# Moving two splits behind an exponential, spreading a check of words, and putting one small product ahead of an output block, in a fused recurrence and feed-forward kernel

## The chip, the cores and the metric

The kernel runs on one core of a Trainium2 chip. The metric is the device time of one execution in microseconds (us). Before the change it takes 355.14 us (median of three runs, 355.14 to 355.28). All comparisons below are between runs that count as fast; a run of a program on one core counts as slow when it is over 1.5% above the fastest of its kernel.

Engines: TensorE (PE, its weight loads PEld), VectorE (DVE), ScalarE (ACT), GpSimd (POOL), SyncE (SP, which here issues nearly all DMAs). The granted clock is the share of TensorE's full clock that the profile records as granted.

## The reference, cut to what matters

```python
for t in range(S):                      # B,H,S,D = 4,8,768,48
    cur = einsum('bhd,bhe->bhde', u[None] * kt, vt)
    y[:, :, t] = einsum('bhd,bhde->bhe', rt, state + cur)
    state = w[None, :, :, None] * state + einsum('bhd,bhe->bhde', kt, vt)
x = y.transpose(0, 2, 1, 3).reshape(B * S, H * D)          # 3072 x 384
h = x @ w_in                                               # 384 -> 1024
e = exp(h - max(h)); sm = e / (sum(e) + 1e-9); solu = h * sm
ln = (solu - mean(solu)) / sqrt(var(solu) + 1e-6) * g_ln
out = ln @ w_out                                           # 1024 -> 384
```

The 3072 rows are cut into N = 24 chunks of 128. The weights come as 64-bit words. The kernel converts them on the chip in a short way that is right only for words of ordinary size, so it reads all words a second time, checks them, and at the end goes a slower general way if the verdict is bad.

Of the kernel before, what the change touches and what calls it, by code (L numbers as in the profile page):

```python
# [399 lines left out]
def direct_path(  # L400
# [64 lines left out]
    def load(i, which="krv"):  # L465
        b, c = units[i]
        for t, src, n in ((kpads, k, "k"), (rpads, r, "r"), (vts, v, "v")):
            if n in which:
                nc.sync.dma_start(out=t[i % len(t)][:, :, 0:D],
                                  in_=src[b, :, ts(c, T), :].rearrange("h s d -> s h d"))  # L470
# [133 lines left out]
    for j in range(8):  # L604
# [5 lines left out]
        else:  # L610
            n = 1 << (j - 1)
# [21 lines left out]
    N = len(units)  # L633
# [3 lines left out]
    def check_sums():  # L637


        L = len(pieces)  # L640
        good = small.tile([128, 2, N + L + HP], F32, name="good", bufs=1)
        low = small.tile([128, 1], F32, name="low", bufs=1)
        nc.vector.tensor_single_scalar(out=good[:, 0, :N], in_=sums, scalar=1.0 / MOST,
                                       op=ALU.is_ge)
        nc.vector.tensor_single_scalar(out=good[:, 1, :N], in_=sums, scalar=MOST, op=ALU.is_le)
        nc.vector.tensor_single_scalar(out=good[:, 0, N : N + L], in_=least, scalar=FLOOR, op=ALU.is_ge)
        nc.vector.tensor_single_scalar(out=good[:, 1, N : N + L], in_=total, scalar=CEIL, op=ALU.is_le)
        nc.vector.tensor_single_scalar(out=good[:, 0, N + L :], in_=decays, scalar=LOW,
                                       op=ALU.is_ge)
        nc.vector.tensor_single_scalar(out=good[:, 1, N + L :], in_=decays, scalar=HIGH,  # L650
                                       op=ALU.is_le)
        nc.vector.tensor_reduce(out=low, in_=good, axis=AX.XY, op=ALU.min)
        n_ps = psH.tile([128, dff], F32, tag="h", name="n_ps")[0:1, 0:1]
        nc.tensor.matmul(n_ps, low, ones, start=True, stop=True)
        nc.vector.tensor_single_scalar(out=bad, in_=n_ps, scalar=127.5, op=ALU.is_lt)
# [10 lines left out]
    def decay_k(i):  # L666
        X = live.setdefault(i, {})
        X["kp"] = apool.tile([128, H, P], F32, name="kp", bufs=5)
        nc.gpsimd.tensor_mul(X["kp"].rearrange("p h d -> p (h d)"),  # L669
                             kpads[i % NLD].rearrange("p h d -> p (h d)"),  # L670
                             kdec.rearrange("p a d -> p (a d)"))
# [78 lines left out]
    def heads(i):  # L750
        b, c = units[i]
        X = live[i]
        vt, AT, St = vts[i % NV], X["AT"], states[b]
        vf = vt.rearrange("p h d -> p (h d)")
        y_ps = psM.tile([128, KD, 128], F32, tag="m", name="y_ps")
        last = {m: n for n, (m, h, at) in enumerate(inner)}
        opened = set()

        def into(m, lhsT, rhs, stop):
            j, g = divmod(m, 4)  # L760
            nc.tensor.matmul(y_ps[32 * g : 32 * g + 32, j, :], lhsT, rhs, start=(g not in opened),  # L761
                             stop=stop, skip_group_check=True)
            opened.add(g)

        if c > 0:
            for m in range(12):
                a, n = divmod(m, 3)
                into(m, St[:, a].rearrange("p q d -> p (q d)")[:, ts(n, 32)], X["rT"][:, a, :],
                     False)
        for n, (m, h, at) in enumerate(inner):  # L770
            into(m, vf[:, at : at + 32], AT[:, h, :], last[m] == n)
        X["y"] = y_ps

    def take_y(i):
        X = live[i]
        X["xT"] = fpool.tile([128, KD, 128], F32, name="xT", bufs=LA + 1)
        nc.scalar.copy(out=X["xT"], in_=X["y"])  # L777

    def outer(chunks):

        chunks = [i for i in chunks if i < N and units[i][1] < C - 1]
        if not chunks:
            return
        kv_ps = psM.tile([128, 2, HP, D], F32, tag="m", name="kv_ps")
        for n, i in enumerate(chunks):
            X, vt = live[i], vts[i % NV]
            X["kv"] = kv_ps[:, n]
            for a in range(HP):
                for g in range(4):
                    h = 2 * a + g // 2  # L790
                    nc.tensor.matmul(X["kv"][ts(g, 32), a], X["kp"][:, h, ts(g % 2, 32)],  # L791
                                     vt[:, h, 0:D], start=True, stop=True)
# [39 lines left out]
    def deviation(i):  # L832
        ss, var, rstd = live[i]["st"]
        live[i]["rstd"] = rstd
        nc.gpsimd.tensor_scalar(out=var, in0=ss, scalar1=1.0 / dff, scalar2=1e-6 * dff ** 2,  # L835
                                op0=ALU.mult, op1=ALU.add)
        nc.gpsimd.tensor_tensor(out=rstd, in0=var, in1=neg_half, op=ALU.pow)
# [4 lines left out]
    def halves():  # L842

        return wpool.tile([128, 2 * 8 * 64, 1], U32, tag="raw", name="halves",
                          bufs=6).bitcast(U16).rearrange("p n o -> p (n o)")

    def split(words):
        return words.bitcast(U16).rearrange("p (n o) -> p o n", o=2)

    def turn(both):  # L850

        turned = halves()
        nc.sync.dma_start(out=turned.rearrange("p (n t) -> p n t", t=128), in_=both,
                          transpose=True)
        return turned.rearrange("p (o n t) -> p o n t", o=2, t=128)
# [5 lines left out]
    def halve_ln(i):  # L861
        X = live[i]
        both = halves()
        nc.scalar.copy(out=both.rearrange("p (o n) -> p o n", o=2), in_=split(X["solu"]))  # L864
        X["turned"] = turn(both)
# [6 lines left out]
    def halve_rk(i):  # L872
        if i < FIRST:
            return
        X = live[i]
        both = halves()
        parts = both.rearrange("p (o e n) -> p o e n", o=2, e=2)
        nc.scalar.copy(out=parts[:, :, 1], in_=split(X["kp"].rearrange("p h d -> p (h d)")))
        nc.vector.tensor_copy(out=parts[:, :, 0], in_=split(X["rp"].rearrange("p h d -> p (h d)")))
        X["turned"] = turn(both)  # L880

    def join_rk(i):
        X = factors(i)
        join(X["rk"].rearrange("p e a t -> p (e a) t"), X["turned"])
# [20 lines left out]
    now = []  # L905
    for i in range(-2, LA + LO):
# [8 lines left out]
        before, now = now, [todo.pop(0) for _ in range(conversions.get(i, 0))]  # L915
# [82 lines left out]
    for i in range(LA + LO, N + LA + LO, 2):  # L998
        j, l = i - LA, i - LA - LO
        for n in (i, i + 1):  # L1000
            if n + 5 < N:
                load(n + 5, "kr")
            if n + 3 < N:
                load(n + 3, "v")
        new = [n for n in (i + 1, i + 2) if FIRST <= n < N]
        late = i == LA + LO
        if late:
            ffn_in(j)
            unit(j)
        for n in (i + 3, i + 4):  # L1010
            if n < N:
                decay_k(n)
                decay_r(n)
                weigh(n, nc.gpsimd)
        for n in (j - 2, j - 1):
            if LO - 1 <= n < N:
                deviation(n)
        if l + 2 < N:
            halve_ln(l + 2)
        for n in new[:1]:  # L1020
            diagonal(n)
        join_ln(l + 1)
        for n in new[:1]:
            join_rk(n)
        if j < N and not late:
            ffn_in(j)
            unit(j)
        if i + 3 < N:
            halve_rk(i + 3)
        for n in new[1:]:  # L1030
            join_rk(n)
        check_next()
        ffn_out(l)
        if l + 3 < N:
            halve_ln(l + 3)
        if j + 1 < N:
            ffn_in(j + 1)
        for n in new[1:]:
            diagonal(n)
        if j + 1 < N:  # L1040
            unit(j + 1)
        if l + 1 == N - 1:
            check_sums()
        ffn_out(l + 1)
        if i + 4 < N:
            halve_rk(i + 4)
        for n in (i + 3, i + 4):
            if n < N:
                sum_own(n)
        now = [n for n in (i + 1, i + 2) if n < N]  # L1050
        for n in now:
            scores(n)
        for n in now:
            take_scores(n)
        now = [n for n in (i, i + 1) if n < N]
        for n in now:
            heads(n)
            take_y(n)
        outer(now)
        for n in now:  # L1060
            update(n)
        if l + 2 < N:
            join_ln(l + 2)
        if i >= N - 1:
            check_next()
    return bad

# [41 lines left out]
```

## The kernel before: the parts that the change touches

From chunk 7 on the chunks go in pairs: twelve iterations with i = 7, 9, ..., 29. In one iteration, rows (scores, y) are at chunks i and i+1, the first product h and its exponential at j = i - 2, and the second product o at l = i - 7. In the traces each engine's work stands in the order in which this loop writes it; in the changed kernel, a split for which ACT waited 3.08 us held up the exponential behind it. A split cuts the 32-bit values of a tile into 16-bit halves, a DMA transposes the halves into a second buffer ("turned"), and a join puts them together again. All these buffers come from one rotation of six.

```python
LA, LO, FIRST = 2, 5, 9
psH = tile_pool(name="psH", bufs=1, space=PSUM)   # h
psM = tile_pool(name="psM", bufs=2, space=PSUM)   # y, kv and o share two buffers

def ffn_in(i):                       # PE: 12 matmuls of 512 columns (h_ps); ACT: exponential
def unit(i):                         # DVE: reciprocal, h*e (solu); ACT: centre, square
def halves():                        # buffers for split words and for turned ones
    return wpool.tile(..., tag="raw", name="halves", bufs=6)
def halve_ln(i):                     # ACT: split rows of solu into 16-bit halves
    both = halves()
    nc.scalar.copy(out=both, in_=split(X["solu"]))
    X["turned"] = turn(both)         # SP: DMA transpose into another buffer
def join_ln(i):                      # DVE: joins the turned halves (lnT)
def halve_rk(i):                     # the same for k (ACT) and r (DVE)
def heads(i): ...                    # PE: y_ps of chunk i from scores and state
def take_y(i):                       # ACT: xT <- y_ps
def ffn_out(i):                      # PE: 16 matmuls (o_ps); ACT: o <- o_ps; SP: store
def check_next():                    # check the piece loaded last, load the next; 14 pieces
    for p in checked: check_words(p) # ACT: abs and its sum; DVE: least of it
    ...
def check_sums(): ...                # DVE: seven small operations; PE: n_ps; DVE: bad

for i in range(LA + LO, N + LA + LO, 2):
    j, l = i - LA, i - LA - LO
    late = i == LA + LO              # the first pair: ffn_in(j), unit(j) come first
    ...                              # cut: loads, decays on POOL, deviation
    if l + 2 < N: halve_ln(l + 2)
    ...                              # cut: diagonal, join_ln(l + 1), join_rk, ffn_in(j), unit(j)
    if i + 3 < N: halve_rk(i + 3)
    ...
    check_next()
    ffn_out(l)
    if l + 3 < N: halve_ln(l + 3)
    if j + 1 < N: ffn_in(j + 1)
    ...                              # cut: diagonal
    if j + 1 < N: unit(j + 1)
    if l + 1 == N - 1: check_sums()
    ffn_out(l + 1)
    if i + 4 < N: halve_rk(i + 4)
    ...                              # cut: scores, take_scores of i + 1, i + 2
    for n in (i, i + 1): heads(n); take_y(n)
    outer(now); update(n)            # kv_ps and the state
    if l + 2 < N: join_ln(l + 2)
    if i >= N - 1: check_next()
```

## Time and profile before

| | before |
|---|---|
| time | 355.14 us |
| TensorE busy | 335.1 us of 354.3 (95%) |
| ACT busy | 241.0 us (68%) |
| one pair in the middle | 26.60 us, TensorE busy for all of it |
| TensorE's waits after the start-up | 1.5 us (n_ps, the verdict), 0.8 us (y_ps), 0.6 us (h_ps), and 0.3 us (kv_ps) for nothing that the profile shows |

The table is read from the bottom up: an engine that is busy for the whole of a pair sets the time there, and the only time that an order of instructions can win is what this engine waits. The prediction shows the lines.

### The profile page before, as it was taken

What the parts mean: (1) busy time and instruction counts of PE and PEld (TensorE: products, weight loads), DVE (VectorE), ACT (ScalarE), POOL (GpSimd) and SP (SyncE); (2) the same over time, 40 slices, a digit from 0 to 9 for tenths busy, and PEclk for the clock granted to TensorE, in tenths of its full rate; (3) what the DMA queues carried; (4) which work ended last, traced back from release to release, by engine and by line L of the source; (5) the groups of instructions that cost most, each with busy time, mean ns of one, the idle gap of its engine ahead of it and who ended that gap; (6) DMA issues with size and microseconds to landing.
All of it is one profiled execution on the core that took longest, in us unless ns stands there. A gap on an engine that the chain in (4) does not pass through costs nothing.

```text
span 354.3 us, 8478 instructions
## 1 busy us (share of the span) xinstructions
PE 335.1 (95%) x3427; PEld 205.5 (58%) x3427; DVE 210.4 (59%) x347; ACT 241.0 (68%) x457; POOL 178.7 (50%) x196
## 2 busy tenths in 40 slices
PE   2699999999999999999999999999999999999983
PEld 2485566655655665575575575575565565555552
DVE  7795888887487468378378378378373252332330
ACT  3765988988878857867867866866867636547520
POOL 3879667789249449449449449449442000000000
PEclk9999999999999999999999999999999999999998
DMA  8999996259999798887999788772973422346941
GB/s 168 264 227 214 245 209 107 51 105 193 199 220 177 177 171 120 185 154 138 187 148 146 185 152 140 186 147 56 174 111 64 97 68 81 85 104 141 213 116 32
DMA packets 164877, 52.76 MB, mean 149 GB/s; under 512 B 157916, under 2 KB 161244, under 8 KB 164828
## 3 DMA queue, kind: packets, MB, share of 16 engines
q1 hardware_dynamic: 164684, 51.92, 76.3%
q8 instruction: 29, 0.48, 0.6%
q10 hardware_dynamic: 144, 0.20, 0.2%
q14 instruction: 20, 0.16, 0.2%
HBM read 26.94 MB, written 4.72 MB: 89 GB/s over the span
## 4 chain that ended last, share of the span: by engine, by line
PE 78%; ACT 9%; DVE 4%; issue 4%; POOL 2%; POOLq 0%; DVEq 0%; ACTq 0%
PE o_ps L896 32%; PE h_ps L814 30%; PE y_ps L761 9%; PE at L728 5%; ACT AT L693 2%; ACT halves L864 2%; PE kv_ps L791 2%; DVE solu L826 2%; ACT solu L828 1%; ACT e L817 1%; ACT e L829 1%; POOL kp L669 1%; PE at L713 1%; POOL rku L682 1%; PE at L705 1%
## 5 line engine op out<-in xcount | busy, mean ns | idle before, releaser
L814 PE MATMUL h_ps<-w_in_sb,xT 128*128 128x512 f32 x288 | 129.0, 597 | 1.2 <-ACT xT L777 0.6
L896 PE MATMUL o_ps<-w_out_sb,lnT 128*128 128x384 f32 (+1 forms) x400 | 127.4, 474 | 0.1
L896 PEld LDWEIGHTS o_ps<-w_out_sb,lnT 128*128 128x128 f32 x400 | 75.0, 190 | 53.3 <-issue 8.6
L814 PEld LDWEIGHTS h_ps<-w_in_sb,xT 128*128 128x128 f32 x288 | 53.5, 190 | 62.5 <-issue 57.4
L804 POOL TENSOR_TENSOR state<-state,pw 64x192 f32<-64x192 f32 x32 | 29.4, 919 | 69.5 <-DVE state L803 67.7
L693 ACT ACTIVATE AT<-ident,own 128x128 f32<-128x128 f32 x192 | 58.6, 391 | 4.7 <-DVE own L687 4.7
L864 ACT COPY halves<-solu 128x2048 uint16<-128x2048 uint16 x24 | 45.4, 1894 | 1.7 <-DMA halves<-halves 1.7
L669 POOL TENSOR_TENSOR kp<-kpad,kdec 128x512 f32<-128x512 f32 x24 | 42.5, 1773 | 7.1 <-ACT kdec L623 6.5
L817 ACT ACTIVATE e<-h_ps 128x1024 f32<-128x1024 f32 x24 | 24.5, 1021 | 29.6 <-PE h_ps L814 29.5
L828 ACT ACTIVATE solu<-solu,st 128x1024 f32<-128x1024 f32 x24 | 27.5, 1146 | 23.7 <-DVE solu L826 23.7
L735 DVE COPY_PREDICATED AT<-later,at 128x512 f32<-128x512 uint32 x48 | 31.6, 729 | 14.9 <-PE at L728 14.9
L824 DVE RECIPROCAL st<-sums 128x1 f32<-128x1 f32 x24 | 3.9, 164 | 60.1 <-ACT e L817 59.9
L858 DVE COPY lnT<-halves 128x2048 uint16<-128x2048 uint16 x24 | 33.8, 1442 | 2.9 <-DMA halves<-halves 2.7
L835 POOL TENSOR_SCALAR st<-st 128x1 f32<-128x1 f32 x24 | 7.2, 298 | 50.2 <-ACT e L829 50.1
L826 DVE SCALAR_TENSOR_TENSOR solu<-h_ps,st,e 128x1024 f32<-128x1024 f32 x24 | 30.8, 1284 | 2.1
L777 ACT COPY xT<-y_ps 128x384 f32<-128x384 f32 x24 | 11.5, 480 | 24.0 <-PE y_ps L761 24.0
L858 DVE COPY rk<-halves 128x2048 uint16<-128x2048 uint16 x15 | 27.5, 1831 | 0.0
L683 POOL TENSOR_TENSOR rku<-rku,rpad 128x384 f32<-128x384 f32 x23 | 26.3, 1143 | 1.8
L761 PE MATMUL y_ps<-AT,vt 128*32 128x128 f32 x768 | 26.3, 279 | 0.0
L728 PE MATMUL at<-rk 48*64 48x128 f32 (+1 forms) x768 | 26.2, 266 | 0.0
L829 ACT ACTIVATE e<-solu 128x1024 f32<-128x1024 f32 x24 | 25.4, 1057 | 0.8
L728 PEld LDWEIGHTS at<-rk 48*64 48x64 f32 x768 | 22.0, 139 | 6.0 <-issue 6.0
(83 smaller groups left out, 336.4 us busy)
## 6 DMA issues: line engine op xcount, KB each, us to landing
raw<-in_moe_w_in_dram SPq DMA_DIRECT2D x12, 512.0 KB, 5.2
raw<-in_moe_w_out_dram SPq DMA_DIRECT2D x16, 384.0 KB, 4.5
kpad<-in_k_dram SPq DMA_DIRECT2D x24, 192.0 KB, 5.0
rpad<-in_r_dram SPq DMA_DIRECT2D x24, 192.0 KB, 5.3
vt<-in_v_dram SPq DMA_DIRECT2D x24, 192.0 KB, 5.2
out_dram<-o SPq DMA_DIRECT2D x23, 192.0 KB, 3.2
halves<-halves SPq DMA_TRANSPOSE x39, 4.7
u_bc<-in_u_dram ACTq DMA_DIRECT2D x1, 192.0 KB, 3.7
```

Of the source, the lines that this page charges most:

```text
L669: nc.gpsimd.tensor_mul(X["kp"].rearrange("p h d -> p (h d)"), kpads[i % NLD].rearrange("p h d -> p (h d)"), kdec.rearrange("p a d -> p (a ...
L693: nc.scalar.activation(out=AT[:, h, :], in_=ident, func=ACT.Copy, scale=X["own"][:, h])
L728: nc.tensor.matmul(ps[q][ts(c, P), a, c * P :], X["kT"][rows, a, ts(c, P)], X["rT"][rows, a, c * P :], start=True, stop=True)
L735: nc.vector.copy_predicated(A4[:, :, q, :], later.to_broadcast([128, HP, T]), live[i]["scores"][q])
L761: nc.tensor.matmul(y_ps[32 * g : 32 * g + 32, j, :], lhsT, rhs, start=(g not in opened), stop=stop, skip_group_check=True)
L804: nc.gpsimd.tensor_mul(S, S, wT)
L814: nc.tensor.matmul(h_ps[:, ts(n, NX)], X["xT"][:, j, :], w_in_sb[:, j, ts(n, NX)], start=(j == 0), stop=(j == KD - 1))
L826: nc.vector.scalar_tensor_tensor(out=solu, in0=X["h"], scalar=rs, in1=X["e"], op0=ALU.mult, op1=ALU.mult, accum_out=tot)
L828: nc.scalar.activation(out=solu, in_=solu, func=ACT.Identity, scale=-float(dff), bias=tot)
L858: nc.vector.tensor_copy(out=words.bitcast(U16).rearrange("p n (t o) -> p o n t", o=2), in_=turned)
L864: nc.scalar.copy(out=both.rearrange("p (o n) -> p o n", o=2), in_=split(X["solu"]))
L896: nc.tensor.matmul(o_ps, X["lnT"][:, f, :], w_out_sb[:, f, part], start=(f == 0), stop=(f == KF - 1))
```

## The change

Its intent is to take those waits away by order alone. (1) The check of words is made twice a pair from the sixth pair on, so that it is done before the end, and the verdict stands ahead of the last output but one. (2) y of the last chunk goes ahead of an output block, which hides its copy by ACT. (3) In the first pair the splits of k, r and rows go behind the second exponential, so that ACT is in time with the output copy for which y waits. No instruction of work is added or removed. The whole diff:

```diff
+        if l + 2 == N:
+            check_sums()
         if l + 2 < N:
             halve_ln(l + 2)
 ...
-        if i + 3 < N:
+        if i + 3 < N and not late:
             halve_rk(i + 3)
 ...
         ffn_out(l)
-        if l + 3 < N:
+        if l + 3 < N and not late:
             halve_ln(l + 3)
 ...
-        if l + 1 == N - 1:
-            check_sums()
+        if i == N - 1:
+            heads(i)
+            take_y(i)
         ffn_out(l + 1)
-        if i + 4 < N:
+        if late:
+            halve_rk(i + 3)
+            halve_ln(l + 3)
+        elif i + 4 < N:
             halve_rk(i + 4)
 ...
-        for n in now:
+        for n in now if i < N - 1 else []:
             heads(n)
             take_y(n)
+        if late:
+            halve_rk(i + 4)
         outer(now)
 ...
-        if i >= N - 1:
+        if i >= N - 7:
             check_next()
```

## The prediction

> **What bounds the kernel now.** I read the head of the page first, then the same figures cut into stretches of one pair of chunks, then the waits of TensorE alone, and last TensorE's timeline around each wait.
>
> ```profile
> PE 335.1 (95%) x3427; PEld 205.5 (58%) x3427; DVE 210.4 (59%) x347; ACT 241.0 (68%) x457; POOL 178.7 (50%) x196
> ...
> 186.60:213.20 26.60, 26.60 (x297) 16.11 (x296) 17.04 (x24) 19.42 (x36) 16.70 (x17) 1.00 0.85 159
> 213.20:239.80 26.60, 26.60 (x297) 16.09 (x296) 17.02 (x24) 19.42 (x36) 16.68 (x17) 1.00 0.81 162
> ```
>
> The columns of the stretches are length, then busy time of PE, PEld, DVE, ACT and POOL, granted clock, DMA share and GB/s. A pair in the middle takes 26.60 us and TensorE is busy for all 26.60; the next engine, ACT, is busy for 19.42. Nothing in the change shortens TensorE's own work, so the middle of the kernel can't gain. Only TensorE's waits can go. All of them:
>
> ```profile
> PE wd_ps L600 <- DVE tab L598: 3.7, 1, 3.7
> PE at L705 <- DMA rpad<-in_r_dram: 2.9, 1, 2.9
> PE at L713 <- POOL kp L669: 1.8, 2, 1.3
> PE n_ps L654 <- DVE low L652: 1.5, 1, 1.5
> PE at L705 <- DVE rku L683: 0.9, 1, 0.9
> PE y_ps L761 <- ACT o L898: 0.8, 1, 0.8
> PE h_ps L814 <- ACT xT L777: 0.6, 1, 0.6
> ```
>
> The reader is to see that three of these seven lines answer to the three parts of the change: n_ps (the verdict on the words, 1.5 us), y_ps behind an output copy (0.8 us), h_ps behind the last xT (0.6 us). The other four lie in the start-up, which the change leaves alone. TensorE's timeline puts the three in their places:
>
> ```profile
> 98.81 0.86 PE L761 MATMUL y_ps<-rk,state 128*32 128x128 f32 x24 [0.78 <-ACT o L898]
> ...
> 310.01 5.42 PE L814 MATMUL h_ps<-w_in_sb,xT 128*128 128x512 f32 x12 [0.60 <-ACT xT L777]
> 315.26 25.96 PE L896 MATMUL o_ps<-w_out_sb,lnT 128*128 128x384 f32 x80
> 342.74 0.19 PE L654 MATMUL n_ps<-ones,low 128*1 128x1 f32 x2 [1.52 <-DVE low L652]
> ```
>
> 0.78 + 0.60 + 1.52 = 2.90 us is the most that the change can take away: 355.14 - 2.90 = 352.24 us.
>
> **What the Trainium skill says.** Perfetto Trace Analysis, section Optimization Strategy, says to find the gaps on the engine that should be saturated and which instruction updates the semaphore that ends each; that is the reading above. TensorE: Matmul & The Clock Gate, Part 2, Step-by-step, says that "The MATMULs themselves stay in program order": a matmul whose operand is late holds up all behind it. The trace agrees: n_ps, 0.19 us of work, held back the last 32 output matmuls for 1.52 us, and moving it in the program's order is a real change. Perfetto Trace Analysis, section Matmuls, says that groups should rotate through PSUM banks so that ACT's or DVE's eviction of one overlaps the next group. Here y, the outputs and kv share a rotation of two buffers, and the 0.78 us is this rotation failing once: y of the second chunk needed the buffer from which ACT had not yet taken an output. DMA: Bandwidth & Descriptors, section Rules for kernel authors, says to issue a DMA early and wait for it late. The checks at the end break that: they have one buffer, and ACT waits 3.36 us for the last words.
>
> **Part 1, the check of words.** No work is added: 14 checks stay 14 (ACT 0.56 + 0.19 us and DVE 0.55 us each). Before, one is made per pair until the last four pairs, so the fourteenth is made in the very last pair. The chain of waits before n_ps:
>
> ```profile
> 341.31 0.55 DVE least L562
> 341.86 0.08 DVE good L643
> ...
> 342.36 0.25 DVE low L652
> 342.61 0.14 issue
> 342.74 0.19 PE n_ps L654 x2
> ```
>
> With two per pair from the sixth pair on, counting the calls gives 5 + 5 x 2 = 15 after the tenth of twelve pairs, which makes all 14. The verdict now stands ahead of the output of chunk 22, the last but one, where it stood ahead of the last: TensorE gets to it after the fourth of the five blocks (5.16 us each) that began at 315.43, so near 336.1 on the old time scale. DVE's last need before it is the join of chunk 22, which ran from 333.18 to 334.50; the seven small operations take from 341.86 to 342.61 when nothing holds them, 0.75 us, to which I add the 0.14 us of issue: 335.4, 0.7 us before TensorE asks. So the whole 1.52 us goes. What it costs: the four earlier checks are spread over five pairs with 26.60 - 19.42 = 7.2 us of free ACT time each, and ACT sat idle 2.02 us before the first exponential of a pair (at 133.85), more than the 0.75 us of a check put ahead of it. Gain: 1.5 us.
>
> **Part 2, count of rows of the last chunk.** TensorE's y of chunk 23 (1.74 us) swaps places with one output block (5.16 us). Before, y ended at 309.42, ACT copied it in 0.48 us, and TensorE waited 0.60. Now y would end near 304.3. ACT is then busy with the second exponential, the centring and the square until 307.76, so the copy is done near 308.3, and TensorE asks for it at about 309.4 when the output block is through. 1.1 us of slack, so all 0.60 us goes. The output block needs the PSUM buffer of the output before it, which ACT took at 297.88: no wait. Gain: 0.6 us.
>
> **Part 3, the first pair.** Before, ACT's order was diagonal (ended 90.1), split of k 1.03, output copy 0.56, split of rows 1.88, exponential at 93.22, and its chain over DVE ended in the output copy at 98.19, for which y waited. With both splits behind the second output copy the exponential starts near 90.6: everything up to that copy moves by 2.6 us less what DVE and TensorE hold, so the copy comes at about 95.7, well before TensorE wants the buffer at 98.03. The 0.78 us goes. But the splits feed DMA transposes, and these now start late. The split of k ends near 97.1, that of rows near 99.0 (before: 93.3). The transpose of rows was issued at 95.41 and took 7.3 us to land, near 102.7, and ACT's next split waited 1.69 us for just that, because it reuses the buffer. Now it is issued near 99.2 to 100, behind that of k. The load of 512 KB for the check, which slowed it before, is by then through; two transposes at 77.38 and 79.44, in a row, took 4.5 and 5.1 us. So it lands at 104 to 105, 1.3 to 2.3 us later than before. From that wait on runs a chain: split 1.9, diagonal 2.44, exponential 1.0, reciprocal and product on DVE, in all 6.8 us (102.78 to 109.54 in the timeline), and the next h_ps may only start after it. Before, h_ps started at 111.58, so the slack was 2.0 us. With TensorE 0.78 us earlier and the chain 1.3 to 2.3 us later, 2.0 - 0.8 - 1.3 = -0.1 up to -1.1 us: a new wait of 0.1 to 1.1, say 0.6. Gain: 0.78 - 0.6 = 0.2 us.
>
> **Sum.** 1.5 + 0.6 + 0.2 = 2.3 us; 355.14 - 2.3 = 352.8 us, 0.7% faster.
>
> **The rivals.** First, that nothing is given back in the first pair: the transposes land by 104.0, and all 2.90 us go, 352.2. For it: the DMA queue has less in it at that moment than before, and a transpose alone took 4.3 to 4.5 us. Against: two go out back to back, and the second waits for the first. Second, that the first pair turns to a loss: a transpose that lands in 7.3 us again lands at 107, the new wait becomes 2 to 3 us, and the kernel ends at 354 to 355. For it: the DMA share is 1.0 and more in those stretches (1.13 from 97 to 100), and a transpose needed that once. Against: the big load no longer stands ahead of it. Third, that the two checks per pair hurt: ACT's queue is in order, and a check waits for its load, which has one buffer and is behind six loads in the queue. If words come late, ACT stands, the exponential is late and TensorE waits in five pairs. Such a load landed in 4.8 us (issued 114.73) and half a pair is 13 us, so I expect nothing; at 0.3 us a pair it would take back 1.5 us and give 354.3. Fourth, that the verdict waits on DVE after all since the join of chunk 22 hangs on a transpose: the slack of 0.7 us would be lost, at most 0.5 us given back.
>
> **Range and chances.** The parts 1 and 2 are read from waits that have a cause which the change takes away, 2.1 us together, and I doubt them by 0.3. Part 3 lies between +0.8 and -1.0. So 352.0 to 353.9 should hold it 8 times in 10. 2% are 7.1 us, more than twice the most that can go, and a loss of 7.1 us would need a wait of 0.6 us in every one of the 12 pairs: within 2% at 0.97, faster 0.01, slower 0.02.
>
> **What would show it.** TensorE's waits after 60 us: the lines of n_ps behind DVE and of h_ps behind xT gone (parts 1 and 2), that of y_ps behind the output copy gone, and in place of it one of h_ps behind DVE's product of 0.1 to 1.1 us near 111 (part 3). Middle pairs still at 26.6 us of TensorE in 26.6. The last word check near 326, no longer at 341. It is wrong if a wait in the middle pairs appears, if n_ps still waits, or if the wait near 111 is over 1.5 us.

## The result, and the profile after

| | before | changed |
|---|---|---|
| median of 4 runs | 355.19 us | 353.09 us |
| range | 355.14 to 355.28 | 352.56 to 353.82 |
| ratio | | 0.9942, 95% interval 0.9924 to 0.9960 |

A ratio is the mean time of one kernel's fast runs over that of the other's of the same rounds, so it is not quite the ratio of the medians. The result is clear of noise, but inside the 2% that count as the same.

The changed kernel's waits of TensorE between 60 and 350 us (in total, times, longest):

```profile
PE h_ps L814 <- DVE solu L826: 0.3, 1, 0.3
PE kv_ps L791 <- issue: 0.2, 1, 0.2
```

The three lines that the change was to remove are gone, and a new one of h_ps behind DVE has come. The kv_ps wait was there before, too (0.3 us). Two stretches of one pair from the middle of the changed kernel, columns as in the prediction:

```profile
184.80:211.40 26.60, 26.60 (x297) 16.19 (x296) 16.99 (x24) 19.42 (x36) 16.62 (x17) 1.00 0.93 165
211.40:238.00 26.60, 26.60 (x297) 16.09 (x296) 17.02 (x25) 19.65 (x37) 16.59 (x18) 1.00 0.79 159
```

The middle is as full as before; with the first added check, in the second of these stretches, ACT goes from 19.42 to 19.65 us of 26.60, and TensorE doesn't notice. TensorE's timeline of the changed kernel, in the first pair and at the end:

```profile
97.36 0.84 PE L761 MATMUL y_ps<-rk,state 128*32 128x128 f32 x24
...
104.93 5.32 PE L896 MATMUL o_ps<-w_out_sb,lnT 128*128 128x384 f32 x16
110.54 5.42 PE L814 MATMUL h_ps<-w_in_sb,xT 128*128 128x512 f32 x12 [0.28 <-DVE solu L826]
115.79 5.32 PE L896 MATMUL o_ps<-w_out_sb,lnT 128*128 128x384 f32 x16
...
303.16 5.43 PE L896 MATMUL o_ps<-w_out_sb,lnT 128*128 128x384 f32 x16
308.43 5.31 PE L814 MATMUL h_ps<-w_in_sb,xT 128*128 128x512 f32 x12
313.58 20.80 PE L896 MATMUL o_ps<-w_out_sb,lnT 128*128 128x384 f32 x64
334.31 0.19 PE L654 MATMUL n_ps<-ones,low 128*1 128x1 f32 x2
334.43 10.63 PE L896 MATMUL o_ps<-w_out_sb,lnT 128*128 128x384 f32 x48
```

y of the second chunk now follows without a gap (97.36), an output block stands between the last y and its h (303.16, then 308.43), and n_ps stands without a wait between two output blocks. The price stands in the third line: h at 110.54 waited for DVE. DVE's side of n_ps:

```profile
325.30 0.55 DVE L562 TENSOR_REDUCE least<-mag 128x1 f32<-128x384 f32 x1 [3.94 <-ACT mag L560]
...
331.51 1.32 DVE L858 COPY lnT<-halves 128x2048 uint16<-128x2048 uint16 x1 [4.02 <-DMA halves<-halves]
...
333.29 0.24 DVE L652 TENSOR_REDUCE low<-good 128x1 f32<-128x84 f32 x1
```

The last word check is at 325.30 instead of 341.31, and the verdict's input is ready at 333.53, 0.78 us before TensorE comes to n_ps.

**The stretches between output blocks.** The starts of the output blocks (16 matmuls each, o_ps) in TensorE's timeline cut an execution into stretches that can be compared between kernels to some hundredths. All profiles:

| kernel | to block 0 | 0 to 2 | 2 to 3 | 3 to 16 | 16 to 18 | 18 to last matmul's end | after it |
|---|---|---|---|---|---|---|---|
| before | 78.73 | 27.69 | 10.31 | 175.38 | 23.15 | 33.07 | 6.00 |
| changed | 78.24 | 26.69 | 10.86 | 175.30 | 22.48 | 31.48 | 5.68 |
| changed, again | 79.02 | 26.69 | 11.00 | 175.46 | 22.48 | 31.48 | 5.54 |
| part 1 alone | 78.65 | 27.67 | 10.31 | 175.10 | 23.15 | 31.48 | 5.77 |
| part 2 alone | 78.44 | 27.67 | 10.31 | 175.89 | 22.48 | 32.99 | 5.87 |
| part 3 alone | 78.33 | 26.69 | 11.06 | 175.65 | 23.15 | 33.08 | 5.41 |
| parts 1 and 2 | 78.40 | 27.67 | 10.31 | 175.37 | 22.48 | 31.48 | 5.34 |
| parts 1 and 2, again | 78.38 | 27.67 | 10.31 | 175.46 | 22.48 | 31.48 | 5.83 |
| rows split first | 79.32 | 26.69 | 15.31 | 174.91 | 22.48 | 31.48 | 5.33 |
| seven buffers | 78.58 | 26.69 | 10.31 | 175.69 | 22.48 | 31.48 | 5.48 |
| only k and r moved | 78.43 | 26.75 | 10.68 | 175.19 | 22.48 | 31.48 | 5.96 |
| verdict in its old place | 78.61 | 26.69 | 11.15 | 175.51 | 22.48 | 32.01 | 5.98 |
| seven buffers, no part 3 | 78.89 | 27.67 | 10.31 | 175.44 | 22.48 | 31.48 | 5.63 |
| two checks from the first pair | 78.50 | 26.69 | 10.84 | 176.85 | 22.48 | 31.48 | 5.83 |

Each part has its own column: part 3 takes 1.00 us from block 0 to 2 and gives 0.55 back from 2 to 3; part 2 takes 0.67 from 16 to 18; part 1 takes 1.59 from the last. Together 1.00 - 0.55 + 0.67 + 1.59 = 2.71 us. The two profiled runs differ by 3.6 us, but 0.49 of it lies before block 0 and 0.32 after the last matmul. Those two columns vary by 1.1 and 0.7 us among kernels that have the same program there, so that is noise. The profiled run of before (356.06 us) was also slower than its timed ones, and that of the changed kernel (352.56) the fastest of its four; by the medians the gain is 2.10 us.

**Where the 0.55 us comes from.** The chain of work that ended last goes through a DMA in the changed kernel (start, length, what):

```profile
98.50 5.07 DMA halves<-halves
...
103.64 1.90 ACT halves L864
105.55 2.35 ACT AT L693 x8
107.89 1.01 ACT e L817 x2
...
109.19 1.30 DVE solu L826 x2
110.49 0.04 issue
110.54 5.42 PE h_ps L814 x12
```

The transpose of the rows is issued at 98.50. ACT waits for it 3.08 us (before: 1.69) with the next pair's first split, here before and after the change:

```profile
102.78 1.90 ACT L864 COPY halves<-solu 128x2048 uint16<-128x2048 uint16 x1 [1.69 <-DMA halves<-halves]
```

```profile
103.64 1.90 ACT L864 COPY halves<-solu 128x2048 uint16<-128x2048 uint16 x1 [3.08 <-DMA halves<-halves]
```

Then come the diagonal, the exponential and DVE's product in order, and only then may TensorE overwrite h. Before, this stretch ended 2.0 us ahead of TensorE.

### The profile page after: what moved, and what is told of

Its sections match the earlier page's. It is cut to its first block, busy times and chain, and to the rows that moved or that the text cites. A ratio compares the mean times of both kernels' runs of the same rounds, so it can differ in the third digit from the quotient of the medians.

```text
span 350.7 us, 8480 instructions
## 1 busy us (share of the span) xinstructions
PE 334.1 (95%) x3427; PEld 204.6 (58%) x3427; DVE 210.7 (60%) x347; ACT 240.3 (69%) x457; POOL 179.0 (51%) x196
## 4 chain that ended last, share of the span: by engine, by line
PE 81%; ACT 7%; DMA 3%; issue 2%; DVE 2%; POOL 2%; SPq 0%; ACTq 0%; POOLq 0%; DVEq 0%
PE o_ps L896 34%; PE h_ps L814 30%; PE y_ps L761 9%; PE at L728 5%; ACT AT L693 3%; ACT halves L864 2%; DVE solu L826 1%; DMA halves<-halves 1%; PE kv_ps L791 1%; ACT e L817 1%; DMA g_sb<-in_moe_g_ln_dram 1%; POOL kp L669 1%; DMA wq<-in_w_dram 1%; ACT solu L828 1%; ACT e L829 1%
## 5 line engine op out<-in xcount | busy, mean ns | idle before, releaser
L804 POOL TENSOR_TENSOR state<-state,pw 64x192 f32<-64x192 f32 x32 | 27.6, 861 | 68.8 <-DVE state L803 67.2
L669 POOL TENSOR_TENSOR kp<-kpad,kdec 128x512 f32<-128x512 f32 x24 | 41.6, 1735 | 6.9 <-ACT kdec L623 6.3
L858 DVE COPY rk<-halves 128x2048 uint16<-128x2048 uint16 x15 | 29.3, 1956 | 0.0
L898 ACT ACTIVATE o<-o_ps,st 128x384 f32<-128x384 f32 (+1 forms) x25 | 13.8, 554 | 18.0 <-PE o_ps L896 11.3
```

The lines of the kernel that those rows point to most:

```text
L669: nc.gpsimd.tensor_mul(X["kp"].rearrange("p h d -> p (h d)"), kpads[i % NLD].rearrange("p h d -> p (h d)"), kdec.rearrange("p a d -> p (a ...
L858: nc.vector.tensor_copy(out=words.bitcast(U16).rearrange("p n (t o) -> p o n t", o=2), in_=turned)
```

## The experiments

**Theory.** Each part takes its own wait away, and nothing comes back except in part 3, where the transposes that are issued late hold a buffer, that buffer holds ACT, and ACT and DVE hold h. **Rivals:** the added checks cost time in the middle; part 1 gains by the new place of the verdict and not by the early checks; what holds h is DVE's joins, or the order of the two splits, and not the buffer.

### The three parts apart

Part 1 alone (check_sums moved, the second check_next from `i >= N - 7`):

> Part 1 alone: two checks of words a pair from the sixth pair on, the verdict ahead of the last output but one. My theory: the wait of n_ps behind DVE (1.52 us) goes and nothing comes in its place; time 355.2 - 1.5 = 353.7 us, the other two waits (0.78 us of y_ps, 0.60 us of h_ps behind xT) stay, middle pairs stay at 26.60 us. Rival (the additional checks hurt the middle pairs by 0.3 us each): about 355.2 us, with waits of TensorE between 170 and 290 us.

Part 2 alone (the heads and take_y of chunk N - 1 ahead of ffn_out):

> Part 2 alone: rows and y of chunk 23 ahead of an output block. My theory: the wait of h_ps behind the last xT (0.60 us) goes, the others stay; 355.2 - 0.6 = 354.6 us. Rival (the wait moves to the output block or comes back behind another copy of ACT): 355.2 us.

Part 3 alone (the three lines with `late`):

> Part 3 alone: both splits of the first pair behind the second exponential. My theory: 0.78 us of y_ps goes, a wait of h_ps behind DVE of some 0.3 us near 111 us comes; the transpose of rows is then in the chain that ends last, and as its landing moves from run to run, the runs scatter by about 1 us, as those of the changed kernel do (352.56 to 353.82); median 354.7 us. Rival A (nothing given back): 354.4 us and a scatter as small as before's (0.14 us). Rival B (given back in full in most runs, the profiled run was a lucky one): 355.2 us or more.

Parts 1 and 2 without part 3:

> Parts 1 and 2 without part 3. My theory: 355.2 - 2.1 = 353.1 us, with a scatter of 0.2 us or less, as before's; so as fast as the whole change in the median and steadier. If part 3 is worth its 0.5 us of the profile in most runs, this is 0.5 us slower than the whole change; if the scatter of the whole change comes from parts 1 and 2, this one scatters by about 1 us too.

Times, all on one chip, where the kernel before took 355.46 us (11 runs, 354.79 to 359.57):

| | median | range | ratio to before | 95% interval |
|---|---|---|---|---|
| part 1 | 354.03 | 353.82 to 354.72 | 0.9946 | 0.9906 to 0.9987 |
| part 2 | 356.33 | 354.53 to 357.85 | 1.0007 | 0.9959 to 1.0055 |
| part 3 | 355.67 | 354.94 to 358.08 | 1.0001 | 0.9955 to 1.0047 |
| parts 1 and 2 | 352.89 | 352.62 to 354.30 | 0.9914 | 0.9872 to 0.9955 |

On this chip the times can't show 0.6 us, and by themselves they would have part 2 worth nothing. The traces can. TensorE's waits between 60 and 350 us, of part 1, part 2 and part 3 in turn:

```profile
PE y_ps L761 <- ACT o L898: 0.8, 1, 0.8
PE h_ps L814 <- ACT xT L777: 0.6, 1, 0.6
```

```profile
PE n_ps L654 <- DVE low L652: 1.4, 1, 1.4
PE y_ps L761 <- ACT o L898: 0.8, 1, 0.8
PE kv_ps L791 <- issue: 0.5, 2, 0.4
```

```profile
PE n_ps L654 <- DVE low L652: 1.5, 1, 1.5
PE h_ps L814 <- ACT xT L777: 0.6, 1, 0.6
PE kv_ps L791 <- issue: 0.5, 1, 0.5
PE h_ps L814 <- DVE solu L826: 0.5, 1, 0.5
```

Each part takes away its own line of the three, and only part 3 brings a wait for another engine. The line of kv_ps comes and goes (none with part 1, 0.5 us with each of the others, none in the second profile of the changed kernel); the last experiment returns to it. The stretches say the same: 1.59, 0.67, and 1.00 less 0.75. So the parts add up, and for the middle the rival falls: part 1 alone has 175.10 us from block 3 to 16 where before has 175.38. All kernels but the last of the table lie between 174.91 and 175.89 there, so the 1.5 us of the rival would have shown.

One expectation was a miss. I thought that the scatter of the changed kernel came from the transpose in its chain, and that without part 3 the runs would agree to 0.2 us. Before scatters by 4.8 us on this chip, and parts 1 and 2 by 1.7. So runs scatter without part 3, too, and where that comes from stays open.

### Is part 3 worth anything, and what gives it back?

The whole change and parts 1 and 2, side by side on another chip:

> The whole change, unaltered, beside its variants on one chip. In its profile: output block 0 to 2 about 26.7 us (before: 27.7), 2 to 3 about 10.9 (before: 10.31), so part 3 nets about 0.45 us; about 352.8 us where before is 355.2. If part 3 is worth nothing in most runs, it equals parts 1 and 2 alone within 0.2 us.

> Parts 1 and 2 again, now beside the whole change on one chip. By the landmarks of the profiles it should be 0.45 us slower than the whole change; if the two are within 0.2 us of each other, part 3 is worth nothing that timing shows.

With the same chip, the splits of k and rows in the other order, and a seventh buffer:

```diff
         if late:
-            halve_rk(i + 3)
             halve_ln(l + 3)
+            halve_rk(i + 3)
```

> The whole change with the two late splits swapped: rows first, then k. Theory A (the wait of ACT is for the transpose of rows and what counts is when that lands): it lands about 2 us sooner, the wait of h_ps behind DVE near 110.5 us goes, blocks 2 to 3 take 10.31 again, 0.5 us faster than the whole change. Theory B (the wait is for the buffer of whichever split was made second, since the buffers go round in turn): the wait stays at about 103.6 us and blocks 2 to 3 stay near 10.9; no difference in time. The waits as compiled speak for B.

```diff
-    def load_weights(j, tag="raw", bufs=6):
+    def load_weights(j, tag="raw", bufs=7):
 ...
         return wpool.tile([128, 2 * 8 * 64, 1], U32, tag="raw", name="halves",
-                          bufs=6)
+                          bufs=7)
```

> The whole change with seven buffers for split and turned halves instead of six, so that the first split of the next pair takes a buffer that the transpose of k frees (landed at 101.6 in the changed kernel) and not that of rows (103.6). My theory: ACT's wait before that split falls from 3.1 us to about 1.1, the wait of h_ps behind DVE near 110.5 goes, blocks 2 to 3 take 10.31, and part 3 gives its full 1.0 us: 0.5 us faster than the whole change, about 352.3 us where before is 355.2. Rival (h_ps is held by DVE's joins of turned halves, which wait for the same transpose): blocks 2 to 3 stay near 10.9.

| | median | range | ratio to before | 95% interval |
|---|---|---|---|---|
| the whole change | 353.44 | 352.87 to 354.38 | 0.9922 | 0.9900 to 0.9944 |
| parts 1 and 2 | 353.57 | 353.42 to 354.75 | 0.9933 | 0.9911 to 0.9955 |
| rows split first | 357.31 | 353.79 to 358.39 | 1.0015 | 0.9976 to 1.0053 |
| seven buffers | 352.55 | 352.15 to 352.74 | 0.9895 | 0.9875 to 0.9914 |

Before took 356.06 us here (11 runs, 355.33 to 357.30). Part 3 as it stands is worth 0.1 us by the medians, and 1.00 - 0.69 = 0.31 us by the stretches of this profile; the intervals overlap, so the times can't tell it from nothing. With the seventh buffer it is worth its full 1.00 us: ACT's first split of the next pair, in the version with seven buffers,

```profile
102.06 1.90 ACT L864 COPY halves<-solu 128x2048 uint16<-128x2048 uint16 x1 [1.17 <-DMA halves<-halves]
```

waited 1.17 us instead of 3.08, h_ps waited for nothing, and blocks 2 to 3 took 10.31 us as before the change. DVE's joins still waited for the transposes there (its last join ran from 106.37 on, and its product began at 108.89), and TensorE did not mind, though with little to spare: the product ended at 110.19 and h started at 110.43. So the buffer was the cause in the changed kernel, and the rival of the joins falls. This version is faster than both kernels: 0.9 us under the whole change and 3.5 us under before, by the medians on this chip.

**Rows first** was meant as a small test and became the largest effect, and neither of its two theories foresaw it. The wait does go with the split that is made second, so theory A falls. But "no difference" was wrong as well. With the longer split ahead, the first transpose was issued at 98.41 and the second only at 101.47 (in the changed kernel 96.47 and 98.50), and ACT's next split came at 107.48 (103.64). Of each of these differences 1.08 us is the later start of block 0 in this profile (79.32 against 78.24); counted from there, the second transpose was issued 1.89 us later. The longer split accounts for 0.86 of that, and the rest is SyncE, which took 2.96 us to issue the first transpose where it took 1.93 in the changed kernel. TensorE's h, and the clock around it (last three columns of the stretches: granted clock, DMA share, GB/s):

```profile
114.37 7.11 PE L814 MATMUL h_ps<-w_in_sb,xT 128*128 128x512 f32 x12 [3.04 <-DVE solu L826]
```

```profile
111.00:114.00 3.00, 0.33 (x2) 0.00 (x0) 1.14 (x2) 1.72 (x5) 3.00 (x4) 1.00 1.41 171
114.00:116.00 2.00, 1.63 (x4) 0.92 (x5) 2.00 (x4) 1.62 (x2) 1.92 (x2) 0.95 1.93 171
116.00:118.00 2.00, 2.00 (x3) 0.73 (x3) 1.27 (x1) 2.00 (x4) 1.92 (x4) 0.50 0.76 154
118.00:120.00 2.00, 2.00 (x4) 0.76 (x3) 0.69 (x1) 2.00 (x4) 0.66 (x2) 0.70 0.83 166
```

The reader is to see the 3.04 us of waiting, and then a granted clock of 0.50. In the other thirteen profiles the clock stays at 1.00 from 25 us to 347 us. The twelve matmuls of h, 5.3 us everywhere else, took 7.11. Of the 5.0 us that blocks 2 to 3 lost (15.31 - 10.31), 1.8 are that slow clock and 3.2 the wait. The Trainium skill has this: TensorE: Matmul & The Clock Gate, section Why this matters for your kernels, asks for no idle gaps of TensorE over some 3 us. Here 3.04 us were enough in the profiled run. Five of the six runs took 356.9 to 358.4 us and one 353.79, and no trace shows why. A clock that did not fall would explain 1.8 us of the 3.1 between it and the next; for the rest, its wait must have been shorter, too. The prediction had a wait of 2 to 3 us as its second rival and would have put it at its length: it costs half as much again.

### Less moved, the verdict left, the buffer alone, more checks

On a third chip, where before took 355.64 us (11 runs, 354.78 to 356.02). Only the splits of k and r moved; the split of rows stays ahead of the exponential:

```diff
-        if l + 3 < N and not late:
+        if l + 3 < N:
             halve_ln(l + 3)
 ...
             halve_rk(i + 3)
-            halve_ln(l + 3)
```

> The whole change, but in the first pair only the splits of k and r go behind the second exponential; the split of rows stays ahead of it. Theory (in part 3 the exponential need move only by the 1.0 us of one split for the output copy to come before 98.0, and the transposes come late only because two follow each other): blocks 0 to 2 take 26.7 as in the change, and 2 to 3 take 10.31 as before, since the transpose that the next pair's split waits for lands near 102.8; 0.5 us faster than the whole change, as with seven buffers. Rival (1.0 us is not enough): y_ps still waits behind the output copy, blocks 0 to 2 near 27.5.

The verdict back in its place, ahead of the last output block, with the checks early:

```diff
-        if l + 2 == N:
-            check_sums()
 ...
+        if l + 1 == N - 1:
+            check_sums()
         ffn_out(l + 1)
```

> The whole change, but the verdict on the words stays ahead of the last output block. Theory A (the gain of part 1 comes from the words being checked early, not from where the verdict stands): n_ps does not wait, the last blocks take what they take in the changed kernel (20.85 + 10.63 = 31.5 us from block 22 less the place of n_ps), no difference in time. Theory B (the place counts): n_ps waits 1 us or more for DVE, whose queue has the join of the last chunk first.

Seven buffers with parts 1 and 2, without part 3:

> Parts 1 and 2 with seven buffers and without part 3: the control for the version with seven buffers. Theory (the seventh buffer only takes away what part 3 gives back, it has no worth of its own): y_ps waits 0.8 us again, blocks 0 to 2 take 27.7 and 2 to 3 10.31, time as parts 1 and 2 alone, 2.4 us under before. Rival (the buffer itself makes the kernel faster): blocks 0 to 2 under 27 us, or the middle pairs faster.

Two checks in every pair:

```diff
-        if i >= N - 7:
-            check_next()
+        check_next()
```

> The whole change, but two checks of words in every pair from the first. Theory (ACT has over 7 us free in a pair, the checks cost TensorE nothing): same time as the whole change, no new wait of TensorE after 130 us. Rival (a check ahead of the first exponential of a pair, or its load of 384 to 512 KB among the six loads, holds up ACT or the transposes): waits of h_ps behind DVE in the early pairs, 0.3 us or more a pair, 1 us slower or more.

| | median | range | ratio to before | 95% interval |
|---|---|---|---|---|
| only k and r moved | 352.61 | 351.86 to 353.12 | 0.9912 | 0.9898 to 0.9927 |
| verdict in its old place | 353.45 | 353.19 to 354.17 | 0.9941 | 0.9928 to 0.9955 |
| seven buffers, no part 3 | 353.18 | 352.92 to 353.72 | 0.9933 | 0.9920 to 0.9947 |
| two checks from the first pair | 354.17 | 353.67 to 354.70 | 0.9961 | 0.9947 to 0.9975 |

*Only k and r moved.* One split is enough for y: blocks 0 to 2 take 26.75 us. But h does not go free as I had expected: 2 to 3 take 10.68. The transpose of k is now issued at 98.49, as late as that of rows was in the change (98.50), since ACT's output copy comes 2 us later; and ACT's next split waits for it:

```profile
103.70 1.90 ACT L864 COPY halves<-solu 128x2048 uint16<-128x2048 uint16 x1 [2.90 <-DMA halves<-halves]
```

So my reason, two transposes in a row, was not the whole of it: what counts is when the last transpose before that buffer is issued. By the stretches this version nets 0.94 - 0.37 = 0.57 us from part 3, a little more than the change. The times on this chip agree: its median is 0.57 us under that of the version with seven buffers and without part 3, which the traces show to be worth as much as parts 1 and 2 alone.

*The verdict in its old place.* TensorE waits again, for less:

```profile
PE n_ps L654 <- DVE low L652: 0.5, 1, 0.5
```

and DVE's timeline of this version says why:

```profile
338.69 1.32 DVE L858 COPY lnT<-halves 128x2048 uint16<-128x2048 uint16 x1 [5.01 <-DMA halves<-halves]
...
340.48 0.24 DVE L652 TENSOR_REDUCE low<-good 128x1 f32<-128x84 f32 x1
```

All words were checked by 326.7, but in DVE's order the join of the last chunk stands ahead of the verdict, and that join waits 5.01 us for its transpose. The last stretch takes 32.01 us, between 33.07 (before) and 31.48 (changed). So theory A and theory B were both too simple: the early checks give 1.06 us and the new place 0.53.

*Seven buffers without part 3* take 27.67 and 10.31 us and have y_ps waiting 0.8 us again. The buffer has no worth of its own; it only spares part 3 its price.

*Two checks from the first pair* are 0.7 us slower than the changed kernel's median by their own ratio (0.9961 against 0.9942, on different chips), and their stretch from 3 to 16 is 1.5 us longer than in the changed kernel. The new wait is neither of those that I had named:

```profile
128.18 0.46 PE L791 MATMUL kv_ps<-vt,kp 128*32 128x48 f32 x22 [1.26 <-issue]
```

Such waits of kv_ps stand in eleven of the fourteen profiles, thirteen of them in all, of 0.16 to 0.54 us and this one of 1.26; "issue" means that nothing in the profile holds it. They come after the 42nd of 64 matmuls near 127 us or after the 44th near 208 us. Before each, a transfer of 16 KB runs on the DMA queue that the profile calls instruction, and in all thirteen the matmul starts 1.26 to 1.49 us after the last packet of it: 127.95 after 126.46 in the kernel before, 126.86 after 125.46 in the changed kernel, 128.18 after 126.88 here. Here that transfer is late, and so are others before it: the load of 512 KB that the added check brings is issued at 104.48, the next two transposes from 113.34 on (111.44 in the changed kernel, which is 0.26 us ahead at block 0), the next load at 119.17 (117.42), and the transfer itself starts at 125.76 (124.01). The timing fits a TensorE that waits for its own instructions behind this traffic, but no run varies that transfer alone, so this is argued and not shown. What is shown: from the sixth pair on the second check is free, and in the early pairs it isn't.

## Why the prediction was right, point by point

- **The total.** 352.8 us were predicted, in a range from 352.0 to 353.9; 353.09 were measured, and the changed kernel's stretches account for 2.71 us against the 2.3 of the sum; the medians say 2.10. To come within 0.3 us of the median is partly luck, since the four runs scatter by 1.3 us; what was right beyond luck is which waits go, and which one comes.
- **Part 1.** 1.5 us predicted, 1.59 measured in the stretch, with the wait of n_ps gone and 0.78 us of slack, of which the 0.14 us of issue leave 0.64, where 0.7 were worked out. The checks cost nothing in the pairs in which the change puts them. What the prediction did not separate is the place of the verdict: a third of the gain hangs on it. It had the cause in its fourth rival (the join that depends on a transpose), but only for the new place, where it did not bite.
- **Part 2.** 0.6 us predicted, 0.67 measured. ACT's copy of y ended at 307.10 and TensorE came to it at 308.43: 1.3 us of slack where 1.1 were worked out.
- **Part 3.** 0.78 us to win and 0.6 to give back were predicted; 1.00 and 0.55 were measured in the profile, 0.53 to 0.84 given back in the others with this order. Counted from block 0, the transpose of rows landed 1.3 us later than before, the low end of the predicted 1.3 to 2.3. The mechanism, from the late transposes over ACT's buffer and the chain to h, was the one that the version with seven buffers proves. The first rival (nothing given back) is what that version shows, and the second (a wait of 2 to 3 us) what the version with rows first shows.
- **The term that was mis-sized** is "0.78 + 0.60 + 1.52 = 2.90 us is the most that the change can take away". The stretches lost 1.00 + 0.67 + 1.59 = 3.26 us. TensorE's idle time before a matmul counts from the end of the last one, and that end is modelled. Before, the last y of the first chunk is listed with an end at 98.03; in the changed kernel the next matmul starts 0.88 us after the start of that group (97.36 - 96.48), so here it could have started at 96.97 + 0.88 = 97.85 and not at 98.03. So a listed wait of 0.78 us cost 1.00. One of 0.28 us cost 0.55: h started 0.45 us late, and 0.10 more passed between its start and the next block's (5.25 us, before 5.15). With only k and r moved, 0.37 us went without any listed wait. The Trainium skill says that the end is an estimate (Perfetto Trace Analysis, section Tensor Engine Instruction); I read it and did not apply it.
- **A reading that was wrong.** The prediction says "All of them" of seven waits, but the view has nine lines. It left out h_ps behind DVE (0.5 us, in the start-up) and kv_ps (0.3 us, at 127.95), which is not in the start-up. Neither belongs to a part of the change, so the sum stands, but the second kind is the one that grew when checks were added to the early pairs.
- **The third rival**, checks that hurt, is true in the pairs where the change does not put them, and by a wait that I had not thought of.

## What to carry to other kernels

When one engine is full in the steady part, list its waits outside that part, and find for each the instruction that ends it; a reordering can win these and no more. Then follow what the reordering makes later: a copy that feeds a DMA transpose holds a buffer until the transpose lands, so moving it back by a few microseconds can meet the next user of that buffer a pair later, and a buffer more may be the cheaper half of the change. Compare traces by the starts of a repeated landmark when the runs scatter by more than the effect.

## What the Trainium skill lacked or had wrong

- Perfetto Trace Analysis, on the Tensor Engine Instruction, says that a matmul's end is estimated, but not which way or by how much. In these runs a listed wait is 0.1 to 0.3 us shorter than the time it costs (0.78 listed, 1.00 lost; 0.60 and 0.67; 0.28 and 0.55).
- DMA: Bandwidth & Descriptors gives a bandwidth of DMA transposes and not their time to landing, which is what decides here: 4.3 us for the quickest of 128 x 2048 two-byte elements, 5.0 to 5.9 for the second of two that are issued 2 to 3 us apart, 7.3 for one issued 1.5 us after a load of 512 KB.
- Runtime: NRT & Kernel Launch, section Instruction fetch mechanics, describes the refill of an engine's instructions in blocks of 16 KB and calls its cost mostly hidden, but gives no size of what is not hidden. If the kv_ps waits are that, which is argued above and not shown, it was 0.16 to 1.26 us in thirteen places of fourteen profiles.
